# Which channels lie on which half of the partitions, and the order in which the second inverse stage is copied out

## The chip, the cores and the metric

The kernel runs on one core of a Trainium2 chip. Its engines work side by side, each through its own queue in order: TensorE (PE, products of matrices, with a weight load beside each), VectorE (DVE), ScalarE (ACT), GpSimd (POOL), and SyncE (SP), which issues transfers. TensorE writes into PSUM, eight banks of 512 floats on each of 128 partitions; ScalarE or VectorE copies from there into SBUF ("eviction"). The metric is the device time of one execution in microseconds; times given are medians over several runs.

## The reference

Two layers over 2048 positions and 512 channels, each a gated long convolution and then an MLP over channels. Cut to what matters:

```
k_shift = sum over t of k_pad[:, t:t+S, :] * shift_k[:, ks-1-t]     # 4 taps
kv      = k_shift * v
y       = irfft(rfft(kv, 2S) * rfft(ssm_k, 2S))[:S] + kv * ssm_D    # along the positions
A(x)    = layernorm(x) * y
B(x)    = gelu(layernorm(x) @ w1 + b1) @ w2 + b2
x = x + A(layernorm(x));  x = x + B(layernorm(x))                   # twice
```

The long convolution y depends on k, v, shift_k, ssm_k and ssm_D alone, and so it is the same in both layers; layernorm of a layernorm is folded into one pass.

## The kernel before, in words

The convolution is written as products with small tables of cosines and sines. The 2048 positions are split into eight residues of 8 and two halves of 1024; the kernel computes half 0 of y, runs both layers on half 0, and in between works out half 1 of y, so that its products and the MLP of half 0 alternate on TensorE. The names that count:

- `stage1`, `stage2`: the forward transforms. Their evictions go through `evac` (line 471), which is a copy on ScalarE (L474) or on VectorE (L475), as a string `ENGS` says for each. Tags are h1, h2 for the filter, x1, x2 for the data, with _0 or _1 for the half.
- The table S2 of `stage2` is spread on the chip at the start: one loaded piece is multiplied by eight masks (columns 8 to 15 of `sg`), one for each of the eight channels of a group. The mask says which rows of the input belong to a channel, so it decides in which order the eight channels of a group come to lie on the 128 partitions, 16 partitions to a channel. Before, this order is 0, 2, 4, 6, 1, 3, 5, 7: even channels on partitions 0 to 63, odd ones on 64 to 127.
- `inverse1`: for each of eight groups j of 64 channels, products of the spectrum (as weights) with the table U. In half 0 (tag i1_0) a product uses all 128 partitions and U's 128 columns. In half 1 (i1_1, `split`) the halves of the partitions are used by two products g = 0 and 1 of 64 rows and 64 columns each, which write into two banks: bank g, and there 16 rows of 32 columns, four for each of eight channel groups i. So a step j is 32 products and one eviction of 128 x 1024. The eviction puts the columns in the order of the channels, 64 neighbouring columns of Z for each j and each of 16 rows that are 512 apart.
- `inverse2` multiplies Z with the table T2 (L710); its evictions give y. It reads all of Z, so it follows the last eviction of inverse1.
- The MLP: L913 is the first product, L918 the gelu on ScalarE, L947 the second product, L951 the sum on VectorE; the norms are L824 (statistics), L829 to L839 on GpSimd and VectorE, L849 and L850 (on ScalarE or VectorE); normed blocks are turned by DMA transposes (L893).

The order of all instructions is written out by hand: `SEQ` is one order of all operations, from which each engine's queue follows, `ENGS` names the engine where two can do it, `BANKS` gives each PSUM tile its bank. In i1_1 all eight evictions are on ScalarE. The tiles of two banks rotate over banks 0 and 1, 2 and 3, 6 and 7, so a step of products waits for an eviction three or fewer steps before it, and groups of MLP products stand between the steps. A wait is put in only where an operand's cells or a bank need it; the cells are four columns wide.

Of the kernel before, what the change touches and what calls it, by code (L numbers as in the profile page):

```python
# [349 lines left out]
def _tables():  # L350

    be = np.arange(128)[:, None]
    k1 = 2 * np.arange(128)[None, :]
    th = TWO_PI * be * (k1 + 0.5) / 256
    F = np.concatenate([np.cos(th), -np.sin(th)], 1)
    a = np.arange(8)
    k2 = np.arange(8)
    f = 2 * np.arange(128)[:, None] + 0.5 + 256 * k2[None, :]
    th = TWO_PI * a[:, None, None] * f[None] / 2048
    c, s = np.cos(th), np.sin(th)  # L360
    S2 = np.zeros((2, 8, 8, 128, 8, 2))
    S2[0, :, :, :, :, 0] = c[:, None]
    S2[1, :, :, :, :, 0] = s[:, None]
    S2[0, :, :, :, :, 1] = -s[:, None]
    S2[1, :, :, :, :, 1] = c[:, None]
    S2 = S2.reshape(128, 2048)
    ph = TWO_PI * k2[:, None] * a[None, :] / 8
    c, s = np.cos(ph), np.sin(ph)
    U = np.zeros((2, 8, 8, 2, 8, 2, 8))
    for d in range(8):  # L370
        U[0, :, d, 0, :, 0, d] = c
        U[1, :, d, 0, :, 0, d] = -c
        U[0, :, d, 0, :, 1, d] = s
        U[1, :, d, 0, :, 1, d] = -s
        U[0, :, d, 1, :, 0, d] = -s
        U[1, :, d, 1, :, 0, d] = -s
        U[0, :, d, 1, :, 1, d] = c
        U[1, :, d, 1, :, 1, d] = c
    U = U[:, :, [0, 2, 4, 6, 1, 3, 5, 7]].transpose(2, 1, 0, 3, 4, 5, 6).reshape(128, 256)
    t = 8 * np.arange(128)[None, :] + a[:, None]  # L380
    ps = TWO_PI * t[None] * (2 * np.arange(128)[:, None, None] + 0.5) / 2048
    T2 = np.stack([np.cos(ps), -np.sin(ps)], 2) / 1024
    T2 = T2.reshape(128, 2048)
    sg = np.where(np.arange(128)[:, None] % 2 == 0, -1.0, 1.0) * np.ones((1, 16))
    sg[:, 8:] = np.arange(128)[:, None] % 8 == np.array([0, 2, 4, 6, 1, 3, 5, 7])
    return F, S2, U, T2, sg


# [4 lines left out]
def bass_interleave_layers__ssm_conv_h3__mixer_channel_mlp__prompt_kernel(  # L393
# [7 lines left out]
    def A(p0, n, off, *dims):  # L401
        return bass.AP(ar, p0 * AR + off, [[AR, n]] + [list(d) for d in dims])
# [4 lines left out]
    def M(p0, n, off, *dims):  # L407
        return bass.AP(sm, p0 * NS + off, [[NS, n]] + [list(d) for d in dims])

    def Q(tile, p0, n, off, *dims):  # L410
        return bass.AP(ps, p0 * 4096 + tile.base * 512 + off, [[4096, n]] + [list(d) for d in dims])
# [12 lines left out]
    def place(n):  # L424
        o = pos[0]
        pos[0] += -(-n // 16) * 16
        return o

    R_ID, R_F, R_SG, R_B1 = place(192), place(256), place(16), place(16)
    R_U, R_DG, R_TC, R_HALO = place(256), place(1024), place(16), place(16)  # L430
# [16 lines left out]
    assert M_MK + 8 <= NS  # L447

    F, S2, U, T2, sg = _tables()
    t_sm = nc.inline_tensor(_bf(np.concatenate([np.eye(128), np.eye(128)[:, :64] + np.eye(128)[:, 64:], F, sg, U, T2], 1)), name="tab_small")  # L450
    t_s2 = nc.inline_tensor(_bf(S2), name="tab_s2")
# [19 lines left out]
    def evac(engs, dst, src, durs, tile):  # L471
        def f(e):
            if e is nc.scalar:
                return e.activation(dst, src(), AF.Copy)  # L474
            return e.tensor_copy(dst, src())  # L475
        return P.op(engs, f, durs, writes=[dst], tile=tile)

    BOTH = (ACT, DVE)
    E1 = {ACT: 912.0, DVE: 1135.0}
# [26 lines left out]
    for h in range(2):  # L506
        for d in range(8):
            o, c, m = A(0, 128, R_S2 + 8192 * h + 16 * d, [128, 64], [1, 16]), A(0, 128, R_C + 1024 * h, [16, 64], [1, 16]), M(0, 128, M_MK + d, [1, 1])
# [12 lines left out]
    tl = Tile(2)  # L521
# [7 lines left out]
    tl = Tile(1)  # L529
# [8 lines left out]
    for i in range(4):  # L538
        o, t = A(0, 128, R_DG + i * 256, [64, 4], [1, 64]), A(0, 128, R_TC + 4 * i, [1, 4], [0, 64])
# [36 lines left out]
    def stage2(G, t):  # L576

        tl = Tile(2)
        ins = [(i, A(0, 128, R_S2 + (16 * t + i) * 128, [1, 128]), A(0, 128, G + (16 * t + i) * 8, [1024, 8], [1, 8])) for i in range(16)]

        def f(e):
            for i, w, m in ins:
                r = e.matmul(Q(tl, 0, 128, i // 8 * 512 + i % 8 * 4, [32, 16], [1, 4]), w, m, start=True, stop=True)  # L583
            return r
        P.op(PE, f, 16 * 30.0, reads=[x for y in ins for x in y[1:]], tile=tl)
        return tl
# [81 lines left out]
    def hap(r, t, d, g=None):  # L668
        return A(0, 128, r + 64 * t + (4096 * g if g else 0), [d, 2], [512, 16 if g is None else 8], [1, 64])

    def inverse1(p, q, Z, split):

        for j in range(8):
            tl = Tile(2)
            ins = []
            for i in range(8):
                dg = 8 * j + i
                for n, r in enumerate((p, q)):
                    o = r + (dg // 4) * 512 + dg % 4
                    if split:  # L680
                        for g in range(2):
                            ins.append((512 * g + 4 * i, n, A(64 * g, 64, o, [4, 128]), A(64 * g, 64, R_U + n * 128 + g, [8, 16], [2, 4])))
                    else:
                        ins.append((i * 128, n, A(0, 128, o, [4, 128]), A(0, 128, R_U + n * 128, [1, 128])))

            def f(e, ins=ins, tl=tl):
                for i, n, w, m in ins:
                    r = e.matmul(Q(tl, 0, 128, i, *([32, 16], [1, 4]) if split else ([1, 128],)), w, m, start=n == 0, stop=n == 1)  # L688
                return r
            P.op(PE, f, 32 * 18.0 if split else 16 * 56.0, reads=[x for y in ins for x in y[2:]], tile=tl)  # L690
            if split:
                evac(BOTH, A(0, 128, Z + 64 * j, [1, 2], [512, 16], [2, 32]),
                     lambda tl=tl: Q(tl, 0, 128, 0, [512, 2], [32, 16], [1, 32]), E1, tl)
                continue
            evac(BOTH, A(0, 128, Z + 64 * j, [512, 16], [8, 8], [1, 8]),
                 lambda tl=tl: Q(tl, 0, 128, 0, [8, 16], [128, 8], [1, 8]), E1, tl)
# [25 lines left out]
    for t in range(8):  # L722
        tl = stage2(R_2, t)
# [17 lines left out]
    for t in range(8):  # L741
        tl = stage2(R_3, t)
# [22 lines left out]
    sg = A(0, 128, R_SG, [1, 1])  # L765
    P.op(POOL, lambda e: e.tensor_copy(SG, sg), 190.0, reads=[sg], writes=[SG])

    P.tag = "i1_0"
    inverse1(R_1, R_2, R_3, False)
    P.tag = "i2_0"  # L770
    inverse2(R_3, R_YT[0])

    P.tag = "h2_1"
    for t in range(8):
        tl = stage2(R_G1, t)
        for g in range(2):
            w = 64 * t + 32 * g
            o, x = A(0, 128, R_3 + w, [512, 16], [1, 32]), A(0, 128, HI + w, [512, 16], [1, 32])
# [7 lines left out]
    for t in range(8):  # L786
        o = hap(R_3, t, D1)
# [10 lines left out]
    for t in range(8):  # L798
        P.tag = "x2_1"
        tl = stage2(R_6, t)  # L800
        xo = R_KT + 1024 * (t % 4)
        evac(BOTH, A(0, 128, xo, [32, 2], [64, 16], [1, 32]), lambda tl=tl: Q(tl, 0, 128, 0, [512, 2], [32, 16], [1, 32]), E1, tl)
        o, p = hap(HH, t, HI - HH), hap(R_3, t, D1)
        tt(o, A(0, 128, xo, [0, 2], [64, 16], [1, 64]), o, ALU.mult, 1137.0)
        P.tag = "sum"
        tt(o, o, p, ALU.add, 1137.0)
    P.tag = "i1_1"
    inverse1(HH, HI, R_Z1, True)
    P.tag = "i2_1"
    inverse2(R_Z1, R_YT[1])  # L810
# [50 lines left out]
    for half in range(2):  # L861
        HTS, XTS, W = R_HT[half], R_XT[half], (256, 512)[half]
        for i in range(2):
            o = A(96, 1, HTS[i] + 10 * W, [1, W])
            P.op(POOL, lambda e, o=o: e.memset(o, 1.0), 100.0 + W, writes=[o])
        for L in range(2):
            s0 = 0
            for n in BLOCKS[half][L]:
# [18 lines left out]
                for i, (xo, yo) in enumerate(sl):  # L887
# [8 lines left out]
                    tl = Tile(1)  # L896
# [9 lines left out]
                for fc in range(11):  # L906
                    rows = 128 if fc < 10 else 96
                    tl = Tile(1)
                    ins = [(A(0, 128, R_W1 + dk * 1376 + fc * 128, [1, rows]), A(0, 128, XTS[k] + dk * W, [1, w])) for dk in range(4)]
# [11 lines left out]
                for i, (xo, yo) in enumerate(sl):  # L921
                    P.tag = "m2"
                    s = ids[i]
                    tl = Tile(1)
                    ins = []
# [62 lines left out]
```

## Time and profile before

| | us |
|---|---|
| median of 3 runs | 242.68 (242.15 to 243.67) |
| the profiled execution | 244.81 |
| its span, first to last instruction | 243.0 |
| TensorE busy | 226.2 (93%) |
| VectorE busy | 183.5 (75%) |
| ScalarE busy | 168.2 (69%) |
| GpSimd busy | 54.1 (22%) |
| chain that ended last: L474 (evictions on ScalarE) | 13% of the span |
| chain that ended last: L688 (products of inverse1) | 3% |
| L474, all 128x1024 copies from float (66) | 65.2 busy, mean 1080 ns |
| L688 in i1_1 (256 products) | 128.5 to 136.5 from the span's start |

How to read it: times of instructions count from the span's start. A line names the start, the length, engine, line of the program, operation, and the form of its operands (partitions x elements). In square brackets stands how long the engine was idle before, and what ended that. The length of an instruction covers its time in the pipeline, so that neighbours on an engine overlap by some 0.1 us on ScalarE, and more on TensorE; the spacing of starts is what an instruction costs its engine. The granted clock was 1.000.

### The profile page before, as it was taken

What the parts mean: (1) busy time and instruction counts of PE and PEld (TensorE: products, weight loads), DVE (VectorE), ACT (ScalarE), POOL (GpSimd) and SP (SyncE); (2) the same over time, 40 slices, a digit from 0 to 9 for tenths busy, and PEclk for the clock granted to TensorE, in tenths of its full rate; (3) what the DMA queues carried; (4) which work ended last, traced back from release to release, by engine and by line L of the source; (5) the groups of instructions that cost most, each with busy time, mean ns of one, the idle gap of its engine ahead of it and who ended that gap; (6) DMA issues with size and microseconds to landing.
All of it is one profiled execution on the core that took longest, in us unless ns stands there. A gap on an engine that the chain in (4) does not pass through costs nothing.

```text
span 243.0 us, 6500 instructions
## 1 busy us (share of the span) xinstructions
PE 226.2 (93%) x2744; PEld 148.4 (61%) x2765; DVE 183.5 (75%) x369; ACT 168.2 (69%) x262; POOL 54.1 (22%) x113
## 2 busy tenths in 40 slices
PE   5898999887999799998999899999999999999996
PEld 1886887885868478685766565754444444444454
DVE  0689989999989799998999699795268787702213
ACT  2689999998988589998969987777318305642620
POOL 2415020006621405026080632203001101100000
DMA  6997367795725820110420202420400050041202
GB/s 190 329 344 212 104 178 217 218 193 112 154 43 138 233 66 4 26 23 12 122 87 3 46 3 43 85 90 0 88 0 3 1 128 1 0 86 46 86 0 89
DMA packets 39097, 23.10 MB, mean 95 GB/s; under 512 B 23478, under 2 KB 33564, under 8 KB 39068
## 3 DMA queue, kind: packets, MB, share of 16 engines
q1 hardware_dynamic: 38770, 22.52, 35.0%
q8 instruction: 22, 0.36, 0.6%
q10 hardware_dynamic: 298, 0.16, 0.3%
q14 instruction: 7, 0.06, 0.1%
HBM read 11.40 MB, written 2.10 MB: 56 GB/s over the span
## 4 chain that ended last, share of the span: by engine, by line
PE 59%; ACT 15%; DVE 15%; POOL 4%; DMA 4%; issue 2%; ACTq 0%; DVEq 0%
PE ps L913 25%; PE ps L947 23%; ACT ar L474 13%; DVE ar L469 5%; PE ps L688 3%; POOL sm L839 3%; DVE sm L824 2%; PE ps L583 2%; DMA ar<-tab_small 2%; PE ps L571 2%; DMA ar<-ar 2%; DVE ar L475 2%; PE ps L554 1%; DVE ar L634 1%; POOL sm L831 1%
## 5 line engine op out<-in xcount | busy, mean ns | idle before, releaser
L918 ACT ACTIVATE ar<-ps,sm 128x256 bf16<-128x256 f32 (+3 forms) x143 | 65.3, 522 | 36.5 <-PE ps L913 34.8
L913 PE MATMUL ps<-ar 128*128 128x256 bf16 (+5 forms) x569 | 83.0, 297 | 1.7 <-DMA ar<-ar 1.3
L947 PE MATMUL ps<-ar 128*128 128x512 bf16 (+1 forms) x325 | 77.5, 379 | 1.6 <-issue 0.5
L474 ACT ACTIVATE ar<-ps 128x1024 bf16<-128x1024 f32 (+3 forms) x76 | 72.3, 1039 | 6.1 <-PE ps L571 2.4
L913 PEld LDWEIGHTS ps<-ar 128*128 128x128 bf16 (+1 forms) x572 | 51.9, 100 | 30.3 <-DMA ar<-ar 1.8
L469 DVE TENSOR_TENSOR ar<-ar 128x512 bf16<-128x512 bf16 (+2 forms) x104 | 63.0, 642 | 6.0 <-ACT ar L849 2.9
L947 PEld LDWEIGHTS ps<-ar 128*128 128x128 bf16 (+1 forms) x341 | 32.4, 98 | 34.7 <-ACT ar L918 0.6
L824 DVE BATCH_NORM_STATS2 sm<-ar 128x6 f32<-128x512 bf16 x64 | 43.0, 683 | 0.4
L951 DVE TENSOR_TENSOR ar<-ar,ps 128x512 bf16<-128x512 bf16 x31 | 20.7, 676 | 28.3 <-PE ps L947 28.2
L849 ACT ACTIVATE ar<-ar,sm 128x512 bf16<-128x512 bf16 x36 | 28.6, 810 | 17.2 <-DVE sm L836 12.3
L831 POOL TENSOR_TENSOR sm<-sm 128x2 f32<-128x2 f32 (+2 forms) x26 | 21.8, 837 | 27.2 <-DVE sm L829 25.4
L829 POOL TENSOR_SCALAR sm<-sm 128x2 f32<-128x2 f32 (+2 forms) x20 | 5.2, 262 | 96.0 <-DVE sm L825 95.6
L571 PE MATMUL ps<-ar 128*64 128x128 bf16 x512 | 20.1, 235 | 1.4 <-ACT ar L474 0.7
L583 PE MATMUL ps<-ar 128*128 128x64 bf16 x512 | 18.6, 193 | 1.8 <-ACT ar L474 1.7
L583 PEld LDWEIGHTS ps<-ar 128*128 128x128 bf16 x512 | 17.0, 98 | 4.6 <-ACT ar L474 3.1
L571 PEld LDWEIGHTS ps<-ar 128*64 128x64 bf16 x512 | 16.8, 119 | 4.9 <-ACT ar L474 1.8
L839 POOL TENSOR_SCALAR sm<-sm 128x1 f32<-128x1 f32 x36 | 17.7, 507 | 1.9
L475 DVE CAST ar<-ps 128x1024 bf16<-128x1024 f32 x12 | 14.5, 1217 | 2.4 <-PE ps L571 1.4
L688 PE MATMUL ps<-ar 64*128 64x64 bf16 (+1 forms) x384 | 12.7, 203 | 1.3 <-ACT ar L474 1.3
L850 DVE TENSOR_SCALAR ar<-ar,sm 128x512 bf16<-128x512 bf16 x28 | 11.2, 411 | 3.5 <-POOL sm L839 2.8
L688 PEld LDWEIGHTS ps<-ar 64*128 64x128 bf16 (+1 forms) x384 | 12.0, 114 | 2.6 <-ACT ar L474 2.2
L781 DVE SCALAR_TENSOR_TENSOR ar<-ar,sm,ps 128x512 bf16<-128x512 bf16 x16 | 11.2, 736 | 0.5 <-PE ps L583 0.5
(45 smaller groups left out, 100.8 us busy)
## 6 DMA issues: line engine op xcount, KB each, us to landing
ar<-ar SPq DMA_DIRECT2D x16, 256.0 KB, 3.6
ar<-in_A_ssm_k_dram SPq DMA_DIRECT2D x8, 256.0 KB, 6.4
ar<-in_A_q_dram SPq DMA_DIRECT2D x8, 256.0 KB, 4.7
ar<-in_A_v_dram SPq DMA_DIRECT2D x8, 256.0 KB, 5.6
out_dram<-ar SPq DMA_DIRECT2D x7, 256.0 KB, 2.3
ar<-in_B_w_dram SPq DMA_DIRECT2D x4, 344.0 KB, 5.9
ar<-in_B_w_dram SPq DMA_DIRECT2D x5, 256.0 KB, 4.7
ar<-in_A_k_dram SPq DMA_DIRECT2D x4, 256.0 KB, 7.1
```

Of the source, the lines that this page charges most:

```text
L469: return P.op(eng, lambda e: e.tensor_tensor(o, a, b, op), dur, reads=[a, b] + list(more), writes=[o])
L474: return e.activation(dst, src(), AF.Copy)
L571: r = e.matmul(Q(tl, 64 * ri, 64, i * 128, [1, 128]), w, m, start=True, stop=True)
L583: r = e.matmul(Q(tl, 0, 128, i // 8 * 512 + i % 8 * 4, [32, 16], [1, 4]), w, m, start=True, stop=True)
L688: r = e.matmul(Q(tl, 0, 128, i, *([32, 16], [1, 4]) if split else ([1, 128],)), w, m, start=n == 0, stop=n == 1)
L824: P.op(DVE, lambda e, sj=sj, x=x: e.bn_stats(sj, x), 600.0, reads=[x], writes=[sj])
L831: P.op(POOL, lambda e: e.tensor_tensor(r, v, hf, ALU.pow), 420.0 + 149.0 * n, reads=[v, hf], writes=[r])
L839: o = e.tensor_scalar(x, y, z, -1.0, ALU.mult, ALU.mult)
L849: return e.activation(o, x, AF.Identity, bias=u, scale=r)
L913: r = e.matmul(Q(tl, 0, rows, 0, [1, w]), a, m, start=dk == 0, stop=dk == 3)
L918: P.op(ACT, lambda e, dst=dst, tl=tl, rows=rows, bias=bias, w=w: e.activation(dst, Q(tl, 0, rows, 0, [1, w]), AF.Gelu_apprx_tanh, bias=bia ...
L947: r = e.matmul(Q(tl, 0, 128, 0, [1, 512]), ins[fc][0], ins[fc][1], start=fc == 0, stop=fc == 10)
```

## The change

The channels of a group lie in their natural order, 0 to 3 on the lower half of the partitions and 4 to 7 on the upper. For that, the rows of U are no longer permuted, and the mask in `sg` has its columns in natural order. In `inverse1` with `split`, product g takes the columns 4g to 4g + 3 of each eight of U, where it took g, g + 2, g + 4, g + 6. Bank g then holds four neighbouring channels of each group of eight instead of every second one. The eviction is turned round with it: it writes 64 neighbouring columns of Z in each of 16 rows, and reads four columns from bank 0, four from bank 1, four from bank 0 and so on; before, it read both banks straight through and wrote every second column, first the even ones, then the odd ones.

```diff
-    U = U[:, :, [0, 2, 4, 6, 1, 3, 5, 7]].transpose(2, 1, 0, 3, 4, 5, 6).reshape(128, 256)
+    U = U.transpose(2, 1, 0, 3, 4, 5, 6).reshape(128, 256)
...
-    sg[:, 8:] = np.arange(128)[:, None] % 8 == np.array([0, 2, 4, 6, 1, 3, 5, 7])
+    sg[:, 8:] = np.arange(128)[:, None] % 8 == np.arange(8)
...
                         for g in range(2):
-                            ins.append((512 * g + 4 * i, n, A(64 * g, 64, o, [4, 128]), A(64 * g, 64, R_U + n * 128 + g, [8, 16], [2, 4])))
+                            ins.append((512 * g + 4 * i, n, A(64 * g, 64, o, [4, 128]), A(64 * g, 64, R_U + n * 128 + 4 * g, [8, 16], [1, 4])))
...
             if split:
-                evac(BOTH, A(0, 128, Z + 64 * j, [1, 2], [512, 16], [2, 32]),
-                     lambda tl=tl: Q(tl, 0, 128, 0, [512, 2], [32, 16], [1, 32]), E1, tl)
+                evac(BOTH, A(0, 128, Z + 64 * j, [512, 16], [1, 64]),
+                     lambda tl=tl: Q(tl, 0, 128, 0, [32, 16], [4, 8], [512, 2], [1, 4]), E1, tl)
                 continue
```

In brackets stand step and count of each dimension, the innermost last. Everything else, the order, the engines and the banks among it, is as it was.

## The prediction

> **What bounds the kernel now.** I read the page first: share of each engine, then the busy digits of TensorE over the span.
>
> ```profile
> span 243.0 us, 6500 instructions
> ...
> PE 226.2 (93%) x2744; PEld 148.4 (61%) x2765; DVE 183.5 (75%) x369; ACT 168.2 (69%) x262; POOL 54.1 (22%) x113
> ...
> PE   5898999887999799998999899999999999999996
> ...
> DVE  0689989999989799998999699795268787702213
> ```
>
> TensorE is busy 93% of the span, and from slice 23 on (6.1 us a slice, so from about 140 us) every digit is 9. Time can only be won where TensorE still waits before that, and only if what follows lets TensorE keep its lead. The change touches the second inverse stage one (tag i1_1), so the second view is the chain of work that ended last, there:
>
> ```profile
> 129.26 4.88 ACT ar L474 x4
> 134.14 0.32 ACT ar L918
> 134.46 4.74 ACT ar L474 x4
> 139.19 0.64 ACT ar L849
> ...
> 146.64 0.37 ACT ar L918
> 147.05 1.48 PE ps L913 x12
> ```
>
> (Start, length, what.) From 129.26 to 139.19 us the chain is ScalarE alone: the eight evictions that the change rewrites, and one gelu. It returns to TensorE at 147.05. So these evictions are on the path. The third view is ScalarE's timeline there, and elsewhere:
>
> ```profile
> 129.26 4.88 ACT L474 ACTIVATE ar<-ps 128x1024 bf16<-128x1024 f32 x4
> 133.96 0.50 ACT L918 ACTIVATE ar<-ps,sm 128x256 bf16<-128x256 f32 x1
> 134.31 4.89 ACT L474 ACTIVATE ar<-ps 128x1024 bf16<-128x1024 f32 x4
> 138.96 0.87 ACT L849 ACTIVATE ar<-ar,sm 128x512 bf16<-128x512 bf16 x1
> ```
> ```profile
> 105.49 2.85 ACT L474 ACTIVATE ar<-ps 128x1024 bf16<-128x1024 f32 x3
> ```
> ```profile
> L474 ACT ACTIVATE ar<-ps x8: 1002/1020/1032, 105.5 to 118.4; 128x1024 bf16<-128x1024 f32 x8
> ```
> ```profile
> 53.04 1.02 ACT L474 ACTIVATE ar<-ps 128x1024 bf16<-128x1024 f32 x1 [0.24 <-PE ps L688]
> ```
> ```profile
> L474 ACT ACTIVATE ar<-ps x8: 1312/1353/1391, 129.3 to 137.8; 128x1024 bf16<-128x1024 f32 x8
> ```
> ```profile
> L474 ACT ACTIVATE ar<-ps x6: 1018/1020/1024, 98.7 to 103.4; 128x1024 bf16<-128x1024 f32 x6
> ```
>
> The rows with three durations are the group of L474 in three windows (minimum, median and maximum in ns). All are 128x1024 copies out of PSUM, but the eight of i1_1 take 1353 ns where others take 1020. Instructions overlap a little, so I price by spacing: (133.96 - 129.26) / 4 = 1.175 us and (138.96 - 134.31) / 4 = 1.163 in i1_1, against (2.85 - 1.03) / 2 = 0.910 at 105 us.
>
> **The change, part by part.**
>
> Tables. U and the mask in sg keep their shapes and their transfers; only values move. The sixteen spread products, the second stages and the swaps have the same operands' shapes. Cost 0, and no cover is needed.
>
> The order and the waits. SEQ, ENGS and BANKS are untouched; the eviction writes the same 1024 cells, the products read the same weights. No wait is added, none removed, and no step moves past another in any queue, SP's and POOL's included.
>
> The eviction's write. Before, it writes 32 elements of every second column; after, 64 neighbours, 16 rows of them. The eight from 105.5 on (x2_1, L802) are the control: they read PSUM with the very pattern that i1_1 has now (1024 in one run), and write in runs of 32 at step 1. Only the step of the write differs, and the price is 0.910 against 1.17. The write of the new form is that of the first inverse (L695), whose last eviction, alone after a wait for L688, is the row at 53.04: 1.02 us. So I take 0.910 for the write.
>
> The eviction's read. After, it takes four columns of one bank, four of the next, and so on. No row has this pattern. Bounds: the six at 98.7 (stage one, L574) read single elements 128 apart, which also changes the bank after every four, and take 1018 to 1024 ns; the first inverse reads runs of eight and takes 1.02. The new pattern lies between these, so the lower end is no cost. The upper end: nothing excludes that a change of bank inside three nested steps costs an element's time on each run: 256 runs of 0.910 / 1024 = 0.89 ns is 0.23 us, which would leave the spacing at 1.14. I take no cost, since both neighbours show none.
>
> So ScalarE has 8 x 0.910 = 7.28 us to do where it had 4.70 + 4.65 = 9.35: 2.07 us less. How much of it reaches TensorE is the real question; its timeline:
>
> ```profile
> 128.49 1.78 PE L688 MATMUL ps<-ar 64*128 64x64 bf16 x96
> 130.66 0.71 PE L688 MATMUL ps<-ar 64*128 64x64 bf16 x32 [0.39 <-ACT ar L474]
> 131.54 0.60 PE L947 MATMUL ps<-ar 128*128 128x512 bf16 x2 [0.16 <-issue]
> 131.97 0.60 PE L913 MATMUL ps<-ar 128*128 128x256 bf16 x4
> 132.41 0.81 PE L947 MATMUL ps<-ar 128*128 128x512 bf16 x3
> 133.16 0.72 PE L688 MATMUL ps<-ar 64*128 64x64 bf16 x32
> 134.19 1.25 PE L688 MATMUL ps<-ar 64*128 64x64 bf16 x64 [0.32 <-ACT ar L474]
> 135.75 0.72 PE L688 MATMUL ps<-ar 64*128 64x64 bf16 x32 [0.30 <-ACT ar L474]
> 136.63 2.54 PE L947 MATMUL ps<-ar 128*128 128x512 bf16 x11 [0.16 <-DVE sm L825]
> 139.25 1.90 PE L710 MATMUL ps<-ar 128*128 128x512 bf16 x8
> ```
> ```profile
> 145.00 3.54 PE L913 MATMUL ps<-ar 128*128 128x256 bf16 x28
> ```
>
> The eight steps of i1_1 are 32 products each: three at 128.49, then one, one, two, one, with MLP products as filler. A step takes 1.25 - 0.72 = 0.53 us of TensorE, and the last product's end shows 0.19 later. From start to start the waits are: 130.27 - 0.19 = 130.08 to 130.66, 0.56 (a normal pitch of 0.02 off); 133.16 + 0.53 = 133.69 to 134.19, 0.50; 134.19 + 1.06 = 135.25 to 135.75, 0.50; the eleven MLP products at 0.216 each from 136.63 reach 139.01, the second inverse stage starts at 139.25, 0.24. Together 1.80 us, all for evictions. The replay at 0.910, with 0.05 from an eviction's end to the product behind it (129.26 + 1.35 = 130.61 to 130.66):
> - Eviction 1 runs 129.26 to 130.28; step 4 starts at 130.33, 0.33 earlier, and ends at 131.05. Evictions 2, 3, 4 start at 130.17, 131.08, 131.99; the fourth ends at 133.01.
> - The filler and step 5 move by 0.33: step 5 starts at 132.83 and ends at 133.55. Steps 6 and 7 need eviction 4 (133.06) and TensorE (132.83 + 0.53 = 133.36): 133.36, 0.83 earlier, no wait left.
> - The gelu takes ScalarE from 132.90 to 133.25; eviction 5 must then wait for step 5 and runs 133.60 to 134.62. TensorE is free at 134.42, so step 8 still waits and starts at 134.67, 1.08 earlier.
> - The filler of eleven starts at 135.55 and ends its slots at 137.93. Evictions 6, 7, 8 start at 134.51, 135.42, 136.33; the last ends at 137.35, before the filler. The second inverse stage starts at 137.93 instead of 139.25: 1.32 us won, and TensorE is the late one.
>
> ScalarE's norm (L849 at 138.96) follows the last eviction: 136.33 + 0.91 = 137.24, 1.72 earlier; its factors are ready:
>
> ```profile
> 136.14 0.62 POOL L839 TENSOR_SCALAR sm<-sm 128x1 f32<-128x1 f32 x2
> 139.86 1.55 DVE L469 TENSOR_TENSOR ar<-ar 128x512 bf16<-128x512 bf16 x4 [2.36 <-ACT ar L849]
> ```
>
> 136.76 on POOL, and VectorE had stood idle 2.36 us for this norm. So the chain norm, VectorE, POOL, norm, gelu, which held TensorE at 147.05, comes 1.72 earlier, TensorE 1.32. What that hold costs: of the 28 products from 145.00 the last twelve (147.05 in the chain) take 1.48 without a wait, four at 131.97 take 0.60, so one more costs (1.48 - 0.60) / 8 = 0.11; 28 should take 1.48 + 16 x 0.11 = 3.24 and took 3.54: 0.30, less than the lead of 0.40 that the chain gets. It goes too. Sum: 1.32 + 0.30 = 1.62 us.
>
> What is late next: TensorE itself. The nearest guard is the group at 158.79, which needs four transposes of SP:
>
> ```profile
> 158.79 1.47 PE L913 MATMUL ps<-ar 128*128 128x256 bf16 x10
> ```
> ```profile
> 152.23 5.12 SPq L893 DMA_TRANSPOSE ar<-ar x4
> DMA to landing us min/median/max: 2.4/2.5/2.5
> ```
>
> The last is issued near 152.23 + 3 x 1.28 = 156.07 and lands at 158.6, 0.2 before use. Its first input comes off the chain that gains 1.72, and its later ones from norms that gain with TensorE, so it should keep ahead; if it stayed where it is, 1.4 of the 1.62 would be lost. Behind it everything hangs on TensorE's own results, and the lead should hold to the end.
>
> The moving operand. The 256 products read four neighbours of U instead of every second of eight. A pair of half-height products now takes 2 x 0.53 / 32 = 33 ns; a full product of 64 columns in runs of eight takes about 30:
>
> ```profile
> 114.83 0.64 PE L583 MATMUL ps<-ar 128*128 128x64 bf16 x16 [0.75 <-ACT ar L474]
> ```
>
> ((0.64 - 0.19) / 15). If the step of two makes the difference, 128 x 3.3 ns = 0.4 us of TensorE falls away, and with steps that still wait for evictions less reaches the end; a loss of the same size cannot be excluded. I take 0 and keep 0.4 on either side.
>
> **A rule against it.** The Trainium skill (SBUF — State Buffer, section on Door 1) says that SBUF is fast as long as consecutive accesses hit the same 16-byte line at least twice. By that rule a write of every second bf16 has four hits in a line and is not slow; then its step is not what costs 0.26 us, and the sum would be 0. Here the trace disagrees: 1353 ns against the control's 1002 to 1032 with the same read. The rule stands as rival one.
>
> **The rivals.** One: the change does nothing. The eight are slow for another reason of that stretch (VectorE's statistics run beside them) or the read gives back what the write wins: 242.7, or with the upper bound above, 0.03 x 8 = 0.2 won, 242.5. For it: no control stands at the same moment. Against: VectorE's digit is 9 both in the slice of 105 us and in that of 129, and at 105 the copies are fast. Two: all of it arrives, 2.07 + 0.30 and the 0.4 of the products: 242.68 - 2.4 = 240.3 and at most 239.9. Against: TensorE has only 1.80 + 0.30 of waits to give, and the replay leaves 0.23 + 0.25 of them. Three, the other side: every change of bank stalls the read. From 0.26 us / 256 runs = 1.0 ns a run it decides against the change; at two elements' time (1.8 ns, 0.46 us an eviction) each costs 1.37, 0.20 more than now, and 8 x 0.20 = 1.6 gives 244.3. Against: the single-element read of stage one, with as many changes, at 1020 ns.
>
> **How the numbers follow.** The profiled execution took 244.81 us with a span of 243.0, 2.1 above the median of 242.68 (242.15 to 243.67); I take the 1.62 off both: span 241.4, median 241.1. Chances: forecast (1.0 to 2.0 won, 240.7 to 241.7) 0.62; small or no gain 0.18 (0.10 of it rival one whole); more than 2.0 won 0.12; slower than now 0.08. The range leaves out the slower case and the edges: 240.2 to 242.9. One per cent, about what a measurement of this kernel can tell from no change, is 2.4 us, more than the largest gain but rival two with the products: faster by over 1% 0.06, within 1% 0.90, slower by over 1% 0.04.
>
> **What would show it.** In the changed profile: the eight copies of i1_1 at about 1020 ns, 0.91 apart where they follow each other; no wait of the two steps at 134.19, which start near 133.4; the second inverse stage near 137.9, after TensorE's own filler; no hold in the 28 products; the group at 158.79 near 157.2. Copies at 1.35 would make it wrong at the write, over 1.14 at the read; fast copies with an end that hasn't moved would make the transposes or a later wait the culprit.

## The result and the profile after

The changed kernel takes 241.15 us (median of 13 runs, 240.31 to 242.74), the kernel before 242.82 (13 runs beside it): ratio 0.9926, 95% interval 0.9900 to 0.9951. It is 0.7% faster, 1.67 us by the medians. Two runs at a much lower granted clock (below, one of 248.05 us at 0.952, and one of 266.35 at 0.853) are left out of every median and ratio.

The profiled execution of the changed kernel took 242.74 us, its span is 240.9 (243.0 before). ScalarE's group of L474 in the window of the stage, with minimum, median and maximum in ns, and ScalarE's timeline there:

```profile
L474 ACT ACTIVATE ar<-ps x8: 1018/1023/1032, 128.9 to 136.0; 128x1024 bf16<-128x1024 f32 x8
```
```profile
133.26 3.78 ACT L474 ACTIVATE ar<-ps 128x1024 bf16<-128x1024 f32 x4
136.93 0.81 ACT L849 ACTIVATE ar<-ar,sm 128x512 bf16<-128x512 bf16 x1
138.22 0.60 ACT L474 ACTIVATE ar<-ps 128x512 bf16<-128x512 f32 x1 [0.48 <-PE ps L710]
```

The eight copies went from 1353 to 1023 ns. The last four follow each other (136.93 - 133.26) / 4 = 0.92 us apart; then ScalarE takes the norm, and after that it is idle for 0.48 us until TensorE delivers the second inverse stage two. Before, TensorE waited for ScalarE there. TensorE's timeline:

```profile
128.16 2.56 PE L688 MATMUL ps<-ar 64*128 64x64 bf16 x128
...
132.50 2.56 PE L688 MATMUL ps<-ar 64*128 64x64 bf16 x128
135.22 2.54 PE L947 MATMUL ps<-ar 128*128 128x512 bf16 x11 [0.16 <-DVE ar L850]
137.59 1.89 PE L710 MATMUL ps<-ar 128*128 128x512 bf16 x8
```
```profile
140.83 1.91 PE L913 MATMUL ps<-ar 128*96 128x256 bf16 x16
142.58 0.81 PE L947 MATMUL ps<-ar 128*128 128x512 bf16 x3
143.23 3.22 PE L913 MATMUL ps<-ar 128*128 128x256 bf16 x28
```
```profile
155.40 0.81 PE L710 MATMUL ps<-ar 128*128 128x512 bf16 x3
...
156.70 1.47 PE L913 MATMUL ps<-ar 128*128 128x256 bf16 x10
```

The steps 1 to 4 now form one row, and 5 to 8 another (after three rows of MLP products): the waits of 0.50 us are gone. Four steps without a wait would take 4 x 0.53 + 0.19 = 2.31 us and take 2.56, so 0.25 is left in each row. It stands before step 4 and before step 8, whose first weight loads, at 130.00 and 134.34, wait for a copy of ScalarE. Three distances, from start to start, tell where the time went:

| | before | after | difference |
|---|---|---|---|
| first product of i1_1 to the second inverse stage two (L688 to the first L710) | 139.25 - 128.49 = 10.76 | 137.59 - 128.16 = 9.43 | -1.33 |
| from there to the last group of L710 | 157.49 - 139.25 = 18.24 | 155.40 - 137.59 = 17.81 | -0.43 |
| span's start to the first product of i1_1 | 128.49 | 128.16 | -0.33 |

(157.49 is the start of the last group of L710 before.) Of the 0.43 the 28 products give 3.54 - 3.22 = 0.32, and the sixteen at 142.50 before, 140.83 now, give 0.10 (2.01 to 1.91). The 0.33 ahead of the stage is not the change's: this distance differs by up to 2.6 us between executions (125.86 to 128.49 us in the profiles of this case at a granted clock of 0.99 or more). So the change is worth 1.33 + 0.43 = 1.76 us in the traces, and 1.67 by the medians. It also arrives whole at the end: from the first product of i1_1 to the end of the span it is 243.0 - 128.49 = 114.5 us before and 240.9 - 128.16 = 112.7 after.

### The profile page after: what moved, and what is told of

Its sections match the earlier page's. It is cut to its first block, busy times and chain, and to the rows that moved or that the text cites. A ratio compares the mean times of both kernels' runs of the same rounds, so it can differ in the third digit from the quotient of the medians.

```text
span 240.9 us, 6500 instructions
## 1 busy us (share of the span) xinstructions
PE 225.8 (94%) x2744; PEld 148.6 (62%) x2765; DVE 183.1 (76%) x369; ACT 166.4 (69%) x262; POOL 54.5 (23%) x113
## 4 chain that ended last, share of the span: by engine, by line
PE 48%; DVE 26%; ACT 9%; POOL 6%; DMA 5%; SPq 4%; issue 2%; DVEq 0%
PE ps L947 21%; PE ps L913 19%; DVE ar L469 10%; ACT ar L474 8%; DVE sm L824 5%; SPq L454 4%; POOL sm L839 3%; DMA ar<-in_A_v_dram 3%; DVE ar L781 3%; PE ps L688 3%; DMA ar<-ar 2%; DVE ar L951 2%; POOL sm L831 1%; DVE ar L475 1%; PE ps L710 1%
## 5 line engine op out<-in xcount | busy, mean ns | idle before, releaser
L913 PE MATMUL ps<-ar 128*128 128x256 bf16 (+5 forms) x569 | 82.8, 297 | 0.7 <-DVE ar L951 0.5
L947 PE MATMUL ps<-ar 128*128 128x512 bf16 (+1 forms) x325 | 77.5, 379 | 1.6 <-issue 0.5
L474 ACT ACTIVATE ar<-ps 128x1024 bf16<-128x1024 f32 (+3 forms) x76 | 70.0, 1005 | 6.1 <-PE ps L710 2.7
L913 PEld LDWEIGHTS ps<-ar 128*128 128x128 bf16 (+1 forms) x572 | 52.0, 100 | 29.0 <-DVE ar L951 0.9
L947 PEld LDWEIGHTS ps<-ar 128*128 128x128 bf16 (+1 forms) x341 | 32.4, 98 | 34.7 <-ACT ar L918 0.6
L839 POOL TENSOR_SCALAR sm<-sm 128x1 f32<-128x1 f32 x36 | 18.2, 518 | 1.9
L688 PEld LDWEIGHTS ps<-ar 64*128 64x128 bf16 (+1 forms) x384 | 11.9, 114 | 1.6 <-ACT ar L474 0.8
L688 PE MATMUL ps<-ar 64*128 64x64 bf16 (+1 forms) x384 | 12.5, 203 | 0.4 <-ACT ar L474 0.3
```

What stands on the lines that cost most here:

```text
L839: o = e.tensor_scalar(x, y, z, -1.0, ALU.mult, ALU.mult)
L913: r = e.matmul(Q(tl, 0, rows, 0, [1, w]), a, m, start=dk == 0, stop=dk == 3)
L947: r = e.matmul(Q(tl, 0, 128, 0, [1, 512]), ins[fc][0], ins[fc][1], start=fc == 0, stop=fc == 10)
```

## The experiments

Theory: a ScalarE write that takes every second bf16 column is slow, whatever surrounds it; only this write is worth anything in the change, and its worth is what the waits behind it were. Rivals: the copies were slow from their neighbours in time; the layout of the channels (table, mask, products) gives part of it; after the change ScalarE still is the limit.

**One element from each bank in turn, in the layout of before.**

```diff
-                evac(BOTH, A(0, 128, Z + 64 * j, [1, 2], [512, 16], [2, 32]),
-                     lambda tl=tl: Q(tl, 0, 128, 0, [512, 2], [32, 16], [1, 32]), E1, tl)
+                evac(BOTH, A(0, 128, Z + 64 * j, [512, 16], [1, 64]),
+                     lambda tl=tl: Q(tl, 0, 128, 0, [32, 16], [1, 32], [512, 2]), E1, tl)
```

> The channels lie as before (every second one on each half, U and the mask as before); only the eviction is turned round: it writes 64 neighbouring columns and reads one element from bank 0, one from bank 1, and so on. My theory, that the step of the write is the whole price and PSUM reads cost the same in any order: the eight copies take 1.02 us, 0.91 apart, second inverse stage at 9.4 us after the first product of the second inverse (10.76 before), time 241.2 as for the change. Rival, that the layout is needed because a read that changes banks at every element is slow: copies over 1.14 us and a time above 242.

The group of L474 in the stage, and two rows of TensorE:

```profile
L474 ACT ACTIVATE ar<-ps x8: 1017/1024/1030, 128.2 to 135.3; 128x1024 bf16<-128x1024 f32 x8
```
```profile
127.47 2.56 PE L688 MATMUL ps<-ar 64*128 64x64 bf16 x128
...
136.90 1.89 PE L710 MATMUL ps<-ar 128*128 128x512 bf16 x8
```

Copies of 1024 ns and a stage of 136.90 - 127.47 = 9.43 us, as with the change. 241.25 us, ratio 0.9931 (0.9909 to 0.9954); the changed kernel on the same chip 241.42, 0.9929 (0.9901 to 0.9957). So the channels didn't have to move at all: turning the eviction round is enough, and a read that changes banks at every element costs ScalarE nothing.

**The changed kernel once more.**

> The changed kernel once more, on the same chip as the three others, as their common measure: 241.15 by the runs so far, ratio 0.993 to before.

That is the 241.42 above. The stage in its profile takes 9.44 us.

**The layout of the change with the write of before.**

```diff
-                evac(BOTH, A(0, 128, Z + 64 * j, [512, 16], [1, 64]),
-                     lambda tl=tl: Q(tl, 0, 128, 0, [32, 16], [4, 8], [512, 2], [1, 4]), E1, tl)
+                evac(BOTH, A(0, 128, Z + 64 * j, [1, 2], [512, 16], [2, 32]),
+                     lambda tl=tl: Q(tl, 0, 128, 0, [512, 2], [32, 16], [1, 32]), E1, tl)
```

> The changed kernel with the eviction of before: U, the mask and the products of the change, the write at step 2 again, so the channels of half 1 come out in another order. My theory: copies of 1.35 us, 1.17 apart, the four waits of TensorE back (0.56, 0.50, 0.50, 0.24 us), 242.8 as before. Rival, that part of the gain comes from the table's neighbouring columns in the products (moving operand) or from the mask: between 241.2 and 242.5, with pairs of products closer than 33 ns.

```profile
126.63 1.79 PE L688 MATMUL ps<-ar 64*128 64x64 bf16 x96
128.80 0.72 PE L688 MATMUL ps<-ar 64*128 64x64 bf16 x32 [0.37 <-ACT ar L474]
...
132.33 1.25 PE L688 MATMUL ps<-ar 64*128 64x64 bf16 x64 [0.31 <-ACT ar L474]
```
```profile
137.38 1.90 PE L710 MATMUL ps<-ar 128*128 128x512 bf16 x8
```

The waits are back, the stage takes 137.38 - 126.63 = 10.75 us, and the time is 242.96, ratio 1.0012 (0.9984 to 1.0039). The products read neighbours of U here, and 96 of them still take 1.79 us where the strided ones took 1.78: the step of the moving operand costs nothing. The rival of the layout falls.

**Half of each copy left out.**

```diff
-                evac(BOTH, A(0, 128, Z + 64 * j, [512, 16], [1, 64]),
-                     lambda tl=tl: Q(tl, 0, 128, 0, [32, 16], [4, 8], [512, 2], [1, 4]), E1, tl)
+                evac(BOTH, A(0, 128, Z + 64 * j, [512, 8], [1, 64]),
+                     lambda tl=tl: Q(tl, 0, 128, 0, [32, 8], [4, 8], [512, 2], [1, 4]), E1, tl)
```

> The changed kernel with only 8 of the 16 rows copied by each of the eight evictions; the other half of the columns is left as it was. My theory, that TensorE bounds the stage after the change but for two waits of 0.25 us: the stage falls from 9.43 to about 8.9 us, the end by 0.5, time 240.65. Rival, that ScalarE still bounds it: eight times 0.43 us less to copy, up to 3.4 us, time towards 238.

```profile
127.25 2.32 PE L688 MATMUL ps<-ar 64*128 64x64 bf16 x128
```
```profile
136.21 1.89 PE L710 MATMUL ps<-ar 128*128 128x512 bf16 x8
```

With copies of 0.6 us the stage takes 136.21 - 127.25 = 8.96 us, 0.47 less than with the change, and the row of four steps is at its 2.31 (2.32 in the trace). The median is 240.27 (6 runs), 1.15 under the changed kernel beside it; the trace gives 0.47 of that in the stage, and the ratio, 0.9893 (0.9865 to 0.9922), has room for it: 0.9929 - 0.47 / 242 = 0.9910. What the rest of the 1.15 is, the traces don't show. In either case eight times 0.43 us less of copying, 3.4 us, did not reach the end: TensorE is the limit after the change, but for two waits of 0.25 for ScalarE.

**Copies alone, by pattern.** A kernel with nothing but copies of 128x1024 floats out of PSUM, four of each pattern on ScalarE, then on VectorE, in one execution. The listing is shortened: A(offset, [step, count], ...) is what is written, in bf16 columns of SBUF; Q(...) is what is read, in floats of PSUM; ONE reads 1024 floats straight through.

```
L64  activation(A(o, [1, 1024]), ONE)                        # step 1
L67  activation(A(o, [1, 2], [512, 16], [2, 32]), ONE)       # the write of before
L70  activation(A(o, [2, 1024]), ONE)                        # L73, L76, L79: steps 4, 8, 16
L82  activation(A(o, [4, 512], [1, 2]), ONE)                 # L85: [8, 256], [1, 4]
L88  activation(A(o, [512, 16], [1, 64]), Q([4, 128], [512, 2], [1, 4]))    # the change
L94  activation(A(o, [1, 1024]), Q([1, 512], [512, 2]))      # L91: runs of 2; L97: step 4
```

> Copies of 128x1024 floats from PSUM to bf16 in SBUF alone, four of each pattern on ScalarE, then on VectorE; nothing else of the kernel is computed. My theory: on ScalarE a write at step 1 costs 0.90 to 0.91 us from start to start, the write of before (step 2 in runs of 32) and step 2 throughout about 1.15, larger steps as much or more; reads cost nothing extra, in runs of four, two or one from two banks, or at step 4. Rival one, that the eight copies were slow from their neighbours in time: step 2 at 0.91 here. Rival two, that 16-byte lines of SBUF count: step 2 and 4 (four and two hits in a line) at 0.91, steps 8 and 16 slower. On VectorE I expect 1.1 for step 1 and the same for the reads; for steps I have no row.

The timeline (four copies in a row, start and length of the whole):

```profile
47.96 3.77 ACT L64 ACTIVATE ar<-ps 128x1024 bf16<-128x1024 f32 x4 [45.95 <-DVE ps L40]
51.76 4.72 ACT L67 ACTIVATE ar<-ps 128x1024 bf16<-128x1024 f32 x4
56.52 4.76 ACT L70 ACTIVATE ar<-ps 128x1024 bf16<-128x1024 f32 x4
61.31 9.22 ACT L73 ACTIVATE ar<-ps 128x1024 bf16<-128x1024 f32 x4
70.56 18.26 ACT L76 ACTIVATE ar<-ps 128x1024 bf16<-128x1024 f32 x4
88.85 17.24 ACT L79 ACTIVATE ar<-ps 128x1024 bf16<-128x1024 f32 x4
106.12 3.77 ACT L82 ACTIVATE ar<-ps 128x1024 bf16<-128x1024 f32 x4
...
113.73 3.77 ACT L88 ACTIVATE ar<-ps 128x1024 bf16<-128x1024 f32 x4
```
```profile
128.94 4.62 DVE L43 CAST ar<-ps 128x1024 bf16<-128x1024 f32 x4 [81.02 <-ACT ar L97]
133.60 4.75 DVE L46 CAST ar<-ps 128x1024 bf16<-128x1024 f32 x4
```

The write of before is slow with no neighbour at all: less a last copy of 1.04 and 1.31 us, the spacing is (3.77 - 1.04) / 3 = 0.91 against (4.72 - 1.31) / 3 = 1.14. The rival of the neighbours falls; in the kernel it was 1.17, so 0.03 may be theirs. The read of the change costs what a straight one does (L88), and so did runs of two, single elements and a step of four (L91, L94, L97: 3.77 each). VectorE hardly minds this write: 4.75 for four against 4.62, 3% where ScalarE pays 25%. But it is not free of the price: at a step of four it needs 9.21 for four copies (L55 on VectorE), as much as ScalarE.

**Other writes alone.** The same kernel with other writes, again one execution, of which these four decided (F(...) is the same memory in floats):

```
L68  activation(A(o + 1, [4, 512], [1, 2]), ONE)   # pairs from an odd column
L71  activation(A(o, [8, 512], [1, 2]), ONE)       # pairs, step 8; L74: step 16
L80  activation(F(o, [1, 1024]), ONE)              # floats; L83: floats at step 2
```

> Copies of 128x1024 floats alone, other writes; nothing else of the kernel is computed. On ScalarE so far: step 1 0.904 us from start to start, step 2 1.13, 4 2.26, 8 4.52, 16 4.27, runs of 2 at step 4 0.904. Theory A, a price for each 4-byte word written, by the distance of the words up to 16 bytes: float at step 1 as bf16 at step 2 (1.1), float at step 2 as bf16 at step 4 (2.2), bf16 at step 3 about 1.7 and at step 6 about 3.3, runs of 2 at step 8 2.2 or half of that, runs of 2 that begin at an odd column slower than 0.904. Theory B, a price for each 16-byte line reached: float at step 1 0.904 to 1.1, runs of 2 at step 16 512 lines x 4.4 ns = 2.2, runs of 4 at step 16 1.1. Both would leave reads of SBUF open: bf16 read at step 2 and 4 from SBUF is measured with them. On VectorE bf16 at step 2 in one run 1.16.

```profile
51.76 6.96 ACT L62 ACTIVATE ar<-ps 128x1024 bf16<-128x1024 f32 x4
58.75 13.74 ACT L65 ACTIVATE ar<-ps 128x1024 bf16<-128x1024 f32 x4
72.52 4.76 ACT L68 ACTIVATE ar<-ps 128x1024 bf16<-128x1024 f32 x4
77.31 3.91 ACT L71 ACTIVATE ar<-ps 128x1024 bf16<-128x1024 f32 x4
81.25 3.98 ACT L74 ACTIVATE ar<-ps 128x1024 bf16<-128x1024 f32 x4
```
```profile
92.87 3.91 ACT L83 ACTIVATE ar<-ps 128x1024 f32<-128x1024 f32 x4
```

Both theories fall. Floats at step 1 cost what bf16 does (L80: 3.77). Floats at step 2 are 8 bytes apart, as bf16 at step 4 is, and cost 3.91 for four, not 9.22; pairs at step 16 reach 512 lines of 16 bytes and cost 3.98, not 8.8. Pairs at step 4 are free from an even column (L82: 3.77) and cost what step 2 costs from an odd one (L68: 4.76). What sorts these rows is whether a write fills whole aligned 4-byte words: if it does, every step tried is nearly free; where each element is half a word, the price grows with the distance. It grows in proportion: four copies take 4.76, 6.96, 9.22, 13.74 and 18.26 us at steps 2, 3 (L62), 4, 6 (L65) and 8, some 2.25 us for each further column; step 16 is out of this line, with 17.24. Why half words are dear is not shown by these runs.

**Which evictions matter.** In the changed kernel, only the first four evictions in ScalarE's order write as before, or only the last four:

```diff
+                if j in (5, 4, 2, 6):        # the other kernel: (7, 1, 3, 0)
+                    evac(BOTH, A(0, 128, Z + 64 * j, [1, 2], [512, 16], [2, 32]),
+                         lambda tl=tl: Q(tl, 0, 128, 0, [512, 2], [32, 16], [1, 32]), E1, tl)
+                    continue
```

> The changed kernel, but the first four evictions of the second inverse's stage one (in ScalarE's order: groups j = 5, 4, 2, 6) write at step 2 as before; the channels of these groups come out in another order. The hand replay of the prediction, with 1.17 us for a slow copy and 0.91 for a fast one: step 4 waits 0.56, steps 6 and 7 wait 0.50, step 8 about 0.1, then TensorE is late; from the first product of the stage to the second inverse stage 10.15 us (10.75 before, 9.43 changed). ScalarE's norm leads by 1.0, TensorE by 0.6, so the hold behind it is gone: from there to the last products of the second inverse stage two 17.8. Time about 1.0 below before. Rival, that the gain is simply in proportion to the fast copies: stage 10.09, and one half of the 1.75.

> The changed kernel, but the last four evictions (j = 7, 1, 3, 0) write at step 2 as before; the channels of these groups come out in another order. By the same replay: step 4 waits 0.24, steps 6 and 7 not, step 8 0.57, the second inverse stage two starts by the last copy, 0.24 after TensorE is free; stage 10.0 us. The norm behind the last copy leads by no more than TensorE, so most of the hold stays: 18.2 from there on. Time about 0.75 below before, less than with the first four slow, though both have four slow copies. Rival, in proportion: as the other one.

TensorE with the first four slow, then with the last four slow (lines behind the edit are four higher, so L714 is L710, L917 is L913):

```profile
125.86 1.78 PE L688 MATMUL ps<-ar 64*128 64x64 bf16 x96
...
136.04 1.89 PE L714 MATMUL ps<-ar 128*128 128x512 bf16 x8
```
```profile
141.68 3.22 PE L917 MATMUL ps<-ar 128*128 128x256 bf16 x28
```
```profile
126.56 2.57 PE L688 MATMUL ps<-ar 64*128 64x64 bf16 x128
...
136.57 1.90 PE L714 MATMUL ps<-ar 128*128 128x512 bf16 x8
```
```profile
142.32 3.54 PE L917 MATMUL ps<-ar 128*128 128x256 bf16 x28
```

Stages of 10.18 and 10.01 us (10.15 and 10.0 expected), the hold of the 28 products gone in the first and whole in the second. So the traces give 0.58 + 0.43 = 1.01 and 0.75, not a half of 1.76 each. The medians were 242.28 (0.999, 0.9963 to 1.0017) and 242.16 (0.9974, 0.9945 to 1.0002): the second as expected, the first half a microsecond short, a miss. It was run again, beside the changed kernel:

> The kernel with the first four evictions slow once more, with more rounds, beside the changed kernel on the same chip: its stage was 10.18 us and 0.57 + 0.43 us are won against before in the trace, but its median lay only 0.5 under that of before. If the trace tells the time: ratio 0.9957, median 0.7 above the changed kernel. If something outside the trace takes it back: 0.999 again.

> The changed kernel as the measure for the two others of this call: ratio 0.993, stage 9.43 us.

Ratio 0.9953 (0.9924 to 0.9981), median 241.86 of eleven runs, against 0.9945 (0.9915 to 0.9974) and 241.28 for the changed kernel. That is 242.96 - 241.86 = 1.10 us under the kernel before, where the trace has 1.01, and 0.58 over the changed kernel, where the traces have 0.75. So the miss was scatter, as far as medians can tell.

A steadier measure than the medians is the stretch from the first product of i1_1 to the end of the span. It is 114.5 and 114.6 us with the write of before (the kernel before, and the old write in the new layout), and 112.7 to 112.8 in four profiles with the new one (the changed kernel three times, the eviction turned round once). With the first four slow it is 239.4 - 125.86 = 113.5, with the last four 240.3 - 126.56 = 113.7: 1.0 and 0.8 less than before, as the replay has it.

**Filler before the waits that are left.** Two places of `SEQ` in the changed kernel: operation 685 (three products of L947) ahead of step 4, and 738 (four of them) ahead of step 8. Where 685 stands in the changed kernel, TensorE's timeline shows two products at 130.88 but three weight loads from 130.65 on, so one record is missing there.

```diff
-  ... 367, 802, 371, 368, 756, 804, 685, 364, ...
+  ... 367, 802, 685, 371, 368, 756, 804, 364, ...
-  ... 805, 365, 859, 806, 807, 769, 738, 366, ...
+  ... 805, 738, 365, 859, 806, 807, 769, 366, ...
```

> The changed kernel with two groups of MLP products moved in TensorE's order: the two products before step 4 and the four before step 8, where TensorE still waits 0.25 us each for an eviction. If the waits fall and the two more turns between long and short products cost nothing, the stage takes 8.95 us as with half copies and the time 240.9; if such a turn costs about 0.2 us (0.34 from the last short product to the next long one, where a normal pitch is 0.02), the stage stays near 9.4. I expect 9.3, and a time that can't be told from the changed kernel's.

```profile
135.67 1.94 ACT L474 ACTIVATE ar<-ps 128x1024 bf16<-128x1024 f32 x2 [0.77 <-PE ps L688]
```
```profile
127.88 1.79 PE L688 MATMUL ps<-ar 64*128 64x64 bf16 x96
...
134.91 0.72 PE L688 MATMUL ps<-ar 64*128 64x64 bf16 x32
135.56 1.90 PE L947 MATMUL ps<-ar 128*128 128x512 bf16 x8
137.66 0.61 PE L710 MATMUL ps<-ar 128*128 128x512 bf16 x2 [0.20 <-ACT ar L474]
```
```profile
145.54 1.48 PE L913 MATMUL ps<-ar 128*128 128x256 bf16 x12 [0.15 <-ACT ar L918]
```

The stage is 137.66 - 127.88 = 9.78 us, 0.35 longer, not shorter; 242.31 us, ratio 0.9963 (0.9937 to 0.9988). Step 8 began 134.91 - 127.88 = 7.03 us into the stage, where the changed kernel has it at 6.18 (132.50 + 2.56 - 0.72 = 134.34, less 128.16). It is copied by the seventh eviction, not the eighth, so ScalarE stood idle 0.77 us for it, and TensorE then waited for the last copy. A wait of 0.25 was traded for a longer one through two engines. The norm behind the last copy came later too, and with it the hold in the products behind it (the row at 145.54): from the first product of i1_1 to the end of the span it is 241.5 - 127.88 = 113.6 us, 0.9 more than with the change, where the medians have 1.03. The 9.3 us expected were a miss. The turn between long and short products was not what cost: the 0.34 us put down to it came from the missing record, and here it is about 0.1 (step 4 starts at 130.35; three products of 0.216 from 129.60 end their slots at 130.25). This one order lost, and no other was tried; with both waits gone, as the half copies have it, the stage is 0.47 us shorter.

## Why the prediction was right

It forecast 241.1 us; 241.15 was measured. That they agree to 0.05 us is luck in part: 1.62 was forecast to be won and 1.67 came by the medians, 1.76 by the traces, and the median of the kernel before went from 242.68 to 242.82 with more runs. The mechanism was the one forecast. By its own steps:

- **The write.** 0.910 was taken from the control with the same read and a write at step 1. The copies came out at 1018 to 1032 ns. Their spacing is (132.71 - 128.92) / 4 = 0.95 and then 0.92, so ScalarE does in 3.79 + 3.67 = 7.46 us what took 9.35: 1.89 less, not 2.07. Most of the 0.18 is the second copy, which starts 1.07 after the first, when the third step, which it copies, is done (128.16 + 3 x 0.53 + 0.19 = 129.94). The write of before alone costs 1.14, so most of the 1.17 was its own; the step of the write was shown by the copies alone and by the old write in the new layout.
- **The read.** Runs of four from two banks were taken as free, bounded by 0.23 us. They are free alone (L88) and in the kernel, and even single elements are.
- **The replay on TensorE.** 1.32 us to the start of the second inverse stage two, 1.33 measured, with waits of 0.25 left before steps 4 and 8 where 0.23 and 0.25 were worked out. It took the evictions in the order of the steps, which is not theirs (the seventh copies step 8); this cost the replay 0.16 on ScalarE and nothing on TensorE, and it is what misled the expectation of the kernel with filler moved.
- **The hold behind it.** 0.30 was forecast, 0.43 came: 0.32 from the 28 products, and 0.10 from the sixteen ahead of them, which a weight load had held up for a copy of ScalarE. In the kernel before, on the timeline of the weight loads:

```profile
143.46 0.77 PEld L913 LDWEIGHTS ps<-ar 128*128 128x128 bf16 x8 [0.20 <-ACT ar L474]
```

  That hold was overlooked, so the term behind the stage was sized too small.
- **The moving operand.** Taken as 0, with 0.4 on either side; it is 0.
- **Where TensorE is full.** The prediction read a 9 in every slice from 140 us on; the last slice has a 6. Nothing hangs on it.
- **The guard.** The transposes were expected to keep ahead of the group at 158.79, and did: it starts 1.30 us after the last group of L710 in both kernels (158.79 - 157.49 and 156.70 - 155.40).
- **The rule.** The Trainium skill (SBUF — State Buffer, Door 1) would have the write of every second bf16 at full speed, with four hits in a line. The runs disagree: 1.14 us against 0.91 alone, and at a step of four, with two hits in a line, 9.22 for four copies against 3.77. It speaks of lines where these rows are sorted by half-filled words.
- **The rivals.** No gain, and a read that stalls at every change of bank, were both excluded; that all that ScalarE wins arrives was excluded by the stage itself (1.33 of it came at once) and by the half copies, which show TensorE as the limit.
- **What can be told.** One per cent was held to be about what can be told from no change; with 13 runs of each kernel, 0.7% was told, at 0.9900 to 0.9951.

## What to carry to other kernels

Where ScalarE copies to bf16, let it write pairs of neighbouring columns that start on an even one, and move the gather to the read from PSUM, which was free in every order tried. On VectorE a step of two cost little here, a step of four as much as on ScalarE. A slow copy is found by comparing rows of one line in several windows: the same form, the same read, one difference. What a faster copy is worth is then the waits of the engine behind it, replayed start by start: 1.89 us less of ScalarE gave 1.33 at once and 0.43 behind.

## What the runs showed of the hardware that was not expected

Four copies of 1024 bf16 per partition take ScalarE 3.77 us at step 1, 4.76 at step 2, and 9.22, 18.26 and 17.24 at steps 4, 8 and 16, in proportion to the step from 2 to 8; but pairs at steps 8 and 16 take 3.91 and 3.98, floats at step 2 take 3.91, and pairs that start at an odd column 4.76. VectorE, which needs 4.62 for four such copies at step 1, shows only 3% at step 2 (in runs of 32, 4.75), but 9.21 and 17.22 at steps 4 and 16. In the kernel the distance from the span's start to this stage differed by 2.6 us between profiles with the same instructions ahead of it, more than the change is worth, while the stretch from there to the end repeated within 0.1 us for kernels with the same write; what makes the first part vary stays open.
